# A spectral filter and two MLP layers on one core: chain results taken a tick later, four results in other buffers, stores and sums moved

## The chip, the core and the metric

One core of a Trainium2 chip runs the whole program in one launch. The metric is the device time of that core in microseconds (us), lower is better; it is given as the median of three runs. Engines are named as the profile names them: PE (TensorE, matmuls), DVE (VectorE), ACT (ScalarE), POOL (GpSimd) and SP (SyncE, which only issues transfers here). Transfers are DMAs, issued from the queues of SP, POOL and, at the very end, ACT.

## The reference, cut to what matters

```python
def _attn_ref(x, filt_r, filt_i):             # x: 2 x 3008 x 256
    X = np.fft.rfft(x, axis=1)
    Y = X * (filt_r + 1j * filt_i)[None, :, :]
    return np.fft.irfft(Y, n=x.shape[1], axis=1).astype(np.float32)

def _moe_ref(x, w_in, w_out):                 # 6016 tokens, 256 -> 2048 -> 256
    h = x @ w_in
    return (h * (1.0 / (1.0 + np.exp(-h)))) @ w_out

def _moe2_ref(x, w_gate, w_val, w_out):       # 256 -> 1536 (two of them) -> 256
    g = x @ w_gate
    return ((g * (1.0 / (1.0 + np.exp(-g)))) * (x @ w_val)) @ w_out
```

The output of the filter, as 6016 tokens of 256, goes through `_moe_ref` (layer 1) and the result through `_moe2_ref` (layer 2).

## The kernel before, in words

Every float32 product is made of three matmuls on operands cut into a high and a low part (`PARTS`): high part by an ACT copy, low part by a DVE subtraction. The Fourier transforms come first, then layer 1, then layer 2. The order of the instructions is written out by hand, and each engine runs its own in that order; the framework places the waits. Tiles rotate in pools: `mid` (33 buffers), `u` (4 buffers, pool `tp`), `late` (9 buffers in layer 2), 8 banks of PSUM. A new tile waits until the buffer that it is given has been read, or stored, for the last time.

**Layer 1, last part.** `Wide` handles blocks of 1024 tokens; its second product is `wide_out`. When the last product of a result is made (`end and k == 1`), the result is copied from PSUM to a `u` tile (line 748, ACT; for `m` = 1 of the last block DVE) and stored to DRAM (line 750, by POOL in the last block). The last block has four of these.

**Layer 2** runs on six blocks of 1024 tokens (the last has 896), each in two halves of columns. A block is six units, a unit is one `Pair`: a gate half `g` and a value half `v`, each a `Gate`, which makes a 2 x 2 block product in seven products instead of eight, with additions around them. The steps of a `Gate` that matter here: `p15` (two products; line 873 copies the bank `a` to the bank `y` on ACT, line 876 copies another to `s5`), `p6` (adds a product to `y`; line 891 copies `y` to a `u` tile `u2`), `p3` (line 901, DVE: bank `b` and `u2` summed), `p7` (line 909, DVE: `c` = `y` + `s5`), `p4` (adds a product to `y`, so it may begin only when line 909 has read `y`). The `p4` of the value half is made at the beginning of the next unit (`tail`), after its `p15`. Lines 1027 to 1051 are the activations and the products of gate and value; line 1045 is DVE's first one in the value half. `side(k)`, with k = -1 to 4, are places in a unit where other work is hung: loads of the next operands, their preparation (`prep_x2`, line 809 on POOL) and splitting (lines 796 and 799), loads of weights (line 648) and the output (`store2`: DVE transposes a result, line 1246, and SP issues four stores of it, line 1249). What `later=True` or `lag` puts off is done at the next `side`.

**Layer 2's output product** is woven into this. Units 2c and 2c + 1 make a chain c, 17 in all; a chain has seven products k in the order `ORDER7` = (3, 1, 7, 5, 2, 6, 4), those of `BACK7` = (3, 7, 4) one chain later, each in two parts p. `tick()` is called seven times in a unit; a tick puts three matmuls of one part in a queue (line 1154), and the queue is emptied between the matmuls of the `Gate`s, at least one for two of those. A tick also makes the casts (`high7`, line 1101, ACT), the low parts one tick later (`lower7`, line 1106, DVE), sums of operands by accumulating DMAs on POOL (`more`, line 1088) and loads of weights on SP (`load7`, line 1115). `after7` takes a finished result out of PSUM as soon as the last of its matmuls has been issued: for k = 1 ACT copies the bank to that of k = 6 (line 1129), for the others DVE adds it to an earlier one (line 1127) or, in the first chain of a block, ACT copies it (lines 1140, 1146). The results collect in the tiles `turned`.

**The end.** The last two units do not fit a chain; `product8` makes their plain products (line 1201) in the order of `AT8` after tick `T0`, in four banks, one for each `m` and `l`. A finished bank is added to `turned` by DVE (line 1207), then transposed and stored on SP and ACT. These last ticks have no other products, so a tick is three matmuls there.

Of the kernel before, what the change touches and what calls it, by code (L numbers as in the profile page):

```python
# [29 lines left out]
P = 128  # L30
# [89 lines left out]
def fft_filter_mlp_kernel(  # L120
# [609 lines left out]
    def wide_out(b, f, h):  # L730

        n = WIDE[b] // 2
        w = wt["o1", f // 4, f % 4 // 2]
        end = f == 15

        def one(m, l, k):
            if f == 0 and k == 0:
                acc[0, b, m, l] = psum("acc")
            a = acc[0, b, m, l][:, :n]
            wpart, xpart = PARTS[k]  # L740
            o = 256 * (f % 2) + 128 * m
            nc.tensor.matmul(  # L742
                a, w[:, wpart, o:o + 128], h[xpart][:, n * l:n * l + n],
                start=(f == 0 and k == 0), stop=(end and k == 1), skip_group_check=True,
            )
            if end and k == 1:
                u = tp.tile([P, 512], F32, tag="u", name="x2")
                (nc.vector.tensor_copy if m and b == len(WIDE) - 1 else nc.scalar.copy)(u[:, :n], a)
                eng = nc.gpsimd if b == len(WIDE) - 1 else nc.sync
                eng.dma_start(d3[NSTD + 2 * b + l][:, m, :n], u[:, :n])  # L750

        queue.extend((one, m, l, k) for m in range(2) for k in (0, 2) for l in range(2))
        queue.extend((one, m, l, 1) for m in range(2) for l in range(2))
# [53 lines left out]
    def prep_x2(t, part):  # L807
        x, n = x2_of[t], size2(t) // 2
        sub = lambda o, a, b: nc.gpsimd.tensor_tensor(o, a, b, op=ALU.subtract)
        if part:  # L810
            x[4] = x[2]
            sub(x[4], x[2], x[6])
            return
        r = sp.tile([P, 2, STEP2 // 2], F32, name="s")
        x[5], x[6], x[7] = x["b12"], r[:, 1, :n], r[:, 0, :n]
        sub(x[7], x[3], x["b12"])
        sub(x[5], x["b12"], x[1])
        sub(x[6], x[3], x[5])
# [331 lines left out]
    def product7(c, k, p, i):  # L1150
        n = size2(c // 3) // 2
        o = bank7(c, k)
        wpart, xpart = PARTS[i]
        nc.tensor.matmul(  # L1154
            o, w7[c, k][:, p, wpart], ops7[c, k, p][:, xpart, :n],
            start=(k in (1, 5) and p == 0 and i == 0), stop=(k in (2, 3, 4) and p == 1 and i == 2),
            skip_group_check=True,
        )
        if p == 1 and i == 2:
            after7(c, k)  # L1160

    T0 = 14 * CHAINS
    AT8 = {}
    for p, first in ((0, (2, 3, 6, 7, 8, 9, 10, 11)), (1, range(14, 22))):
        for x, (v, l) in enumerate(((0, 0), (0, 1), (1, 1), (1, 0))):
            for m in range(2):
                AT8[T0 + first[2 * x + m]] = p, v, l, m
    HIGH8 = {}
    for p, first in ((0, (-4, -3, -2, -1)), (1, (2, 3, 4, 5))):
        for x, (v, l) in enumerate(((0, 0), (0, 1), (1, 1), (1, 0))):  # L1170
            HIGH8[T0 + first[x]] = p, v, l

    def raw8(p, v, l):
# [20 lines left out]
    def product8(p, v, l, m, i):  # L1194
        t = NBLK2 - 1
        n = size2(t) // 2
        o = bank(4 + 2 * l + m)[:, :n]
        wpart, xpart = PARTS[i]
        w = w7["8", {(0, 0): 1, (1, 0): 2, (1, 1): 4, (0, 1): 8}[v, m]]
        end = p == 1 and v == (1 if l == 0 else 1)  # L1200
        nc.tensor.matmul(
            o, w[:, p, wpart], ops7["8", p, v, l][:, xpart, :n],
            start=(p == 0 and v == 0 and i == 0), stop=(end and i == 2), skip_group_check=True,
        )
        if end and i == 2:
            a = turned[t, m][:, l, :n]
            nc.vector.tensor_tensor(a, o, a, op=ALU.add)
            store2(t, m, l, (nc.sync, nc.scalar))

    def tick():  # L1210
        i = clock[0]
# [18 lines left out]
        for when, k, j in SUMS:  # L1230
            for p in range(2):
                c, r = divmod(i - when[p], 14)
                if r == 0 and 0 <= c < CHAINS:
                    more(c, k, j, p)
        for r, o in enumerate((-2, 3, 9, 21)):
            c, x = divmod(i - o, 14)
            if x == 0 and 0 <= c < CHAINS:
                load7(c, r)

    turned = {}  # L1240

    def store2(t, m, l, engines=(nc.sync,)):

        n = size2(t) // 2
        o = tp.tile([P, 512], F32, tag="u", name="ob")
        nc.vector.transpose(o[:, :n], turned[t, m][:, l, :n])
        r0 = STEP2 * t + n * l
        for i in range(4):
            engines[i % len(engines)].dma_start(
                out[r0:r0 + n, P * m + 32 * i:P * m + 32 * i + 32].rearrange("(j r) c -> r j c", r=32),  # L1250
                o[32 * i:32 * i + 32, :n].rearrange("p (j c) -> p j c", c=32),
            )


    units = [(1, t, 4 * q + f) for q in range(4) for t in range(2) for f in range(4)]
# [104 lines left out]
    later(0, -1, split_x2, 0, 7)  # L1360
    later(0, 0, split_x2, 0, 4)
    for t in range(1, NBLK2):
        for n, k, m, l in ((3, 2, 0, 0), (3, 4, 0, 1), (4, 2, 1, 1), (5, 2, 1, 0)):
            later(6 * t + n, k, store2, t - 1, m, l)
        u = 6 * t - 6
        later(u + 2, 0, load_x2, t)
# [3 lines left out]

        for k, n in ((1, 2), (4, 3)):
            later(u + 5, k, split_x2, t, n, True)
        later(u + 5, 3, prep_x2, t, 1)
        later(u + 6, -1, split_x2, t, 7, True)
        later(u + 6, 0, split_x2, t, 4, True)

# [32 lines left out]
    with tc.manual_schedule():  # L1409
# [196 lines left out]
        old.finish()  # L1606
        while clock[0] < T0 + 22:
            tick()
            drain(0)


# [39 lines left out]
```

## Time and profile before

| | us |
|---|---|
| median of three runs (1142.25 to 1142.97) | 1142.68 |
| the profiled execution, its own time | 1142.41 |
| its span, first to last instruction | 1140.6 |
| PE busy | 1112.0 |
| DVE busy | 847.0 |
| ACT busy | 773.1 |
| POOL busy | 399.6 |

The page of the profile is one execution. Busy shares are means over stages of different kinds; what ends a stage is seen in the waits (who waited for whom, summed) and in the timeline (instructions in order of time, with the idle time before one and what ended it in brackets). A matmul is drawn longer than the distance to the next one, since they are pipelined. Layer 2 begins at about 590 us; a block is about 89 us, a unit 14 to 15.

### The profile page before, as it was taken

What the parts mean: (1) busy time and instruction counts of PE and PEld (TensorE: products, weight loads), DVE (VectorE), ACT (ScalarE), POOL (GpSimd) and SP (SyncE); (2) the same over time, 40 slices, a digit from 0 to 9 for tenths busy, and PEclk for the clock granted to TensorE, in tenths of its full rate; (3) what the DMA queues carried; (4) which work ended last, traced back from release to release, by engine and by line L of the source; (5) the groups of instructions that cost most, each with busy time, mean ns of one, the idle gap of its engine ahead of it and who ended that gap; (6) DMA issues with size and microseconds to landing.
All of it is one profiled execution on the core that took longest, in us unless ns stands there. A gap on an engine that the chain in (4) does not pass through costs nothing.

```text
span 1140.6 us, 15418 instructions
## 1 busy us (share of the span) xinstructions
PE 1112.0 (97%) x4999; PEld 912.7 (80%) x4999; DVE 847.0 (74%) x1310; ACT 773.1 (68%) x1459; POOL 399.6 (35%) x375
## 2 busy tenths in 40 slices
PE   9999999999999999999998999999999999999996
PEld 7588888998888887888886778778878877887885
DVE  5887465566676686787564788888888888888886
ACT  5788766766676677676564776776676676676662
POOL 3557826544522363352101322322322312322220
PEclk9999999999999999999998999999999999999999
DMA  9974443427254455453673668799799799799794
GB/s 244 289 236 119 135 139 115 145 100 247 100 185 155 151 197 182 148 185 120 212 264 133 137 155 236 180 231 242 172 228 242 193 225 232 201 227 229 194 241 95
DMA packets 146977, 212.70 MB, mean 186 GB/s; under 512 B 58704, under 2 KB 88016, under 8 KB 146896
## 3 DMA queue, kind: packets, MB, share of 16 engines
q1 hardware_dynamic: 125280, 179.26, 49.6%
q0 software_dynamic: 17456, 31.79, 16.2%
q10 hardware_dynamic: 4160, 0.66, 0.3%
q8 instruction: 40, 0.66, 0.2%
q14 instruction: 41, 0.34, 0.1%
HBM read 138.20 MB, written 42.73 MB: 159 GB/s over the span
## 4 chain that ended last, share of the span: by engine, by line
PE 86%; DVE 7%; DMA 3%; ACT 2%; issue 1%; POOL 0%; SPq 0%; DVEq 0%; ACTq 0%
PE bk L840 25%; PE acc L742 15%; PE bk L1154 12%; PE acc L719 7%; PE h L669 6%; PE y L840 6%; PE xb L840 4%; PE xa L840 4%; DMA w<-d 3%; PE s L209 2%; PE s L397 2%; PE s L206 2%; PE s L282 1%; DVE ho L1106 1%; DVE u L901 1%
## 5 line engine op out<-in xcount | busy, mean ns | idle before, releaser
L840 PE MATMUL bk<-xo,wst 128*128 128x512 f32 (+1 forms) x864 | 279.3, 388 | 6.0 <-ACT u L891 3.9
L742 PE MATMUL acc<-h,w 128*128 128x512 f32 x768 | 283.7, 389 | 0.0
L1154 PE MATMUL bk<-ho,w 128*128 128x512 f32 (+1 forms) x714 | 265.5, 388 | 2.0 <-DMA w<-d 2.0
L840 PE MATMUL bk<-xo,w 128*128 128x512 f32 (+1 forms) x648 | 211.7, 393 | 9.4 <-DVE c L909 8.7
L840 PEld LDWEIGHTS bk<-xo,wst 128*128 128x128 f32 x864 | 162.7, 189 | 40.9 <-ACT u L891 4.6
L742 PEld LDWEIGHTS acc<-h,w 128*128 128x128 f32 x768 | 144.2, 188 | 29.6
L1088 POOL DMA_DIRECT2D ga<-c x68 | 59.4, 1063 | 297.1 <-DVE ho L1106 290.4
L1154 PEld LDWEIGHTS bk<-ho,w 128*128 128x128 f32 x714 | 133.9, 188 | 28.4 <-DMA w<-d 4.5
L840 PEld LDWEIGHTS bk<-xo,w 128*128 128x128 f32 x648 | 120.7, 189 | 42.5 <-DVE c L909 18.6
L1106 DVE TENSOR_TENSOR ho<-ga,ho 128x512 fp32r<-128x512 f32 (+1 forms) x136 | 95.2, 701 | 0.6 <-ACT ho L1101 0.6
L719 PE MATMUL acc<-h,w 128*128 128x512 f32 (+1 forms) x384 | 95.4, 376 | 0.0
L1101 ACT CAST ho<-ga 128x512 fp32r<-128x512 f32 (+1 forms) x136 | 82.3, 615 | 6.7 <-PE bk L840 5.3
L669 PE MATMUL h<-xh,w 128*128 128x512 f32 (+1 forms) x248 | 83.6, 379 | 0.1
L719 PEld LDWEIGHTS acc<-h,w 128*128 128x128 f32 x384 | 71.2, 188 | 11.2
L873 ACT COPY bk<-bk 128x512 f32<-128x512 f32 (+1 forms) x72 | 40.7, 566 | 58.0 <-PE bk L840 44.7
L1106 DVE TENSOR_TENSOR ho<-c,ho 128x512 fp32r<-128x512 f32 (+1 forms) x102 | 76.5, 750 | 0.9 <-ACT ho L1101 0.6
L677 DVE TENSOR_TENSOR h<-h,h 128x512 fp32r<-128x512 f32 (+1 forms) x64 | 41.4, 655 | 47.9 <-ACT h L676 46.5
L840 PE MATMUL xb<-xo,wst 128*128 128x512 f32 x192 | 74.7, 391 | 1.6 <-DVE h L936 1.6
L840 PE MATMUL xa<-xo,w 128*128 128x512 f32 x192 | 75.6, 395 | 0.0
L840 PE MATMUL y<-xo,wst 128*128 128x512 f32 x192 | 74.7, 389 | 0.0
L891 ACT COPY u<-bk 128x512 f32<-128x512 f32 (+1 forms) x72 | 41.8, 581 | 40.0 <-PE bk L840 35.2
L901 DVE TENSOR_TENSOR u<-bk,u 128x512 f32<-128x512 f32 (+1 forms) x72 | 48.6, 676 | 18.8 <-PE bk L840 17.4
(165 smaller groups left out, 2193.6 us busy)
## 6 DMA issues: line engine op xcount, KB each, us to landing
w<-d SPq DMA_DIRECT2D x53, 512.0 KB, 4.7
wst<-ds_g SPq DMA_DIRECT2D x36, 512.0 KB, 4.8
wst<-ds_v SPq DMA_DIRECT2D x36, 512.0 KB, 5.1
wst<-ds SPq DMA_DIRECT2D x32, 512.0 KB, 4.6
ga<-c POOLq DMA_DIRECT2D x60, 256.0 KB, 5.6
c<-ga POOLq DMA_DIRECT2D x30, 256.0 KB, 9.1
zt<-d SPq DMA_DIRECT2D x16, 384.0 KB, 5.2
d<-z SPq DMA_DIRECT2D x11, 512.0 KB, 4.4
```

The lines of the kernel that those rows point to most:

```text
L669: nc.tensor.matmul(ps[:, :n], wt[key, f // 4, g][:, wpart, o:o + P], x[xpart][:, g, :n], start=(g == 0 and k == 0), stop=(g == 1 and k == 2),)
L677: nc.vector.tensor_tensor(h[:, 1, :n], u[:, :n], h[:, 0, :n], op=ALU.subtract)
L719: nc.tensor.matmul(a[:, :n], w[:, wpart, o:o + 128], h[:, xpart, :n], start=(f == 0 and k == 0), stop=(f == 15 and k == 2),)
L742: nc.tensor.matmul(a, w[:, wpart, o:o + 128], h[xpart][:, n * l:n * l + n], start=(f == 0 and k == 0), stop=(end and k == 1), skip_group_c ...
L840: nc.tensor.matmul(o, w(wpart), x[:, xpart, :o.shape[-1]], start=(first and k == 0), stop=(last and k == 2), skip_group_check=True,)
L873: nc.scalar.copy(self.y, self.a)
L891: nc.scalar.copy(self.u2, self.y)
L901: nc.vector.tensor_tensor(self.u2, self.b, self.u2, op=ALU.add)
L1088: nc.gpsimd.dma_start(o, v, accum_op=ALU.add)
L1101: nc.scalar.copy(x[:, 0, :v.shape[-1]], v)
L1106: nc.vector.tensor_tensor(x[:, 1, :n], v, x[:, 0, :n], op=ALU.subtract)
L1154: nc.tensor.matmul(o, w7[c, k][:, p, wpart], ops7[c, k, p][:, xpart, :n], start=(k in (1, 5) and p == 0 and i == 0), stop=(k in (2, 3, 4) ...
```

## The change

1. Last block of layer 1: the four results go to `mid` tiles instead of `u` tiles.
2. `after7` is called from the next `tick()` (list `taken`), behind that tick's casts, low parts and sums, and ahead of its loads, instead of straight after the last matmul of a result.
3. `store2` in the blocks but the last: the transposition is put one place of the unit earlier, and the four stores are put off to the next place (`lag`), that is, they stay where they were.
4. `prep_x2`'s last subtraction goes from POOL to DVE and from place 3 to place 4 of its unit.
5. The first load of a chain's weights is issued one tick earlier (-3 instead of -2).
6. The end: the columns' halves are done in the order `ORDER8`; the earlier sum is added to the bank in PSUM (`join8`) between its first and its last products, and the transposition reads the bank.

```diff
--- before.py
+++ after.py
@@ -744,7 +744,10 @@
                 start=(f == 0 and k == 0), stop=(end and k == 1), skip_group_check=True,
             )
             if end and k == 1:
-                u = tp.tile([P, 512], F32, tag="u", name="x2")
+                if b == len(WIDE) - 1:
+                    u = mid([P, 2, 512], "x2")[:, 0]
+                else:
+                    u = tp.tile([P, 512], F32, tag="u", name="x2")
                 (nc.vector.tensor_copy if m and b == len(WIDE) - 1 else nc.scalar.copy)(u[:, :n], a)
                 eng = nc.gpsimd if b == len(WIDE) - 1 else nc.sync
                 eng.dma_start(d3[NSTD + 2 * b + l][:, m, :n], u[:, :n])
@@ -809,7 +812,7 @@
         sub = lambda o, a, b: nc.gpsimd.tensor_tensor(o, a, b, op=ALU.subtract)
         if part:
             x[4] = x[2]
-            sub(x[4], x[2], x[6])
+            nc.vector.tensor_tensor(x[4], x[2], x[6], op=ALU.subtract)
             return
         r = sp.tile([P, 2, STEP2 // 2], F32, name="s")
         x[5], x[6], x[7] = x["b12"], r[:, 1, :n], r[:, 0, :n]
@@ -1157,17 +1160,20 @@
             skip_group_check=True,
         )
         if p == 1 and i == 2:
-            after7(c, k)
+            taken.append((c, k))
+
+    taken = []
 
     T0 = 14 * CHAINS
     AT8 = {}
+    ORDER8 = ((0, 1), (1, 1), (0, 0), (1, 0))
     for p, first in ((0, (2, 3, 6, 7, 8, 9, 10, 11)), (1, range(14, 22))):
-        for x, (v, l) in enumerate(((0, 0), (0, 1), (1, 1), (1, 0))):
+        for x, (v, l) in enumerate(ORDER8):
             for m in range(2):
                 AT8[T0 + first[2 * x + m]] = p, v, l, m
     HIGH8 = {}
     for p, first in ((0, (-4, -3, -2, -1)), (1, (2, 3, 4, 5))):
-        for x, (v, l) in enumerate(((0, 0), (0, 1), (1, 1), (1, 0))):
+        for x, (v, l) in enumerate(ORDER8):
             HIGH8[T0 + first[x]] = p, v, l
 
     def raw8(p, v, l):
@@ -1197,15 +1203,18 @@
         o = bank(4 + 2 * l + m)[:, :n]
         wpart, xpart = PARTS[i]
         w = w7["8", {(0, 0): 1, (1, 0): 2, (1, 1): 4, (0, 1): 8}[v, m]]
-        end = p == 1 and v == (1 if l == 0 else 1)
+        end = p == 1 and v == 1
         nc.tensor.matmul(
             o, w[:, p, wpart], ops7["8", p, v, l][:, xpart, :n],
             start=(p == 0 and v == 0 and i == 0), stop=(end and i == 2), skip_group_check=True,
         )
         if end and i == 2:
-            a = turned[t, m][:, l, :n]
-            nc.vector.tensor_tensor(a, o, a, op=ALU.add)
-            store2(t, m, l, (nc.sync, nc.scalar))
+            store2(t, m, l, (nc.sync, nc.scalar), o)
+
+    def join8(m, l):
+        t = NBLK2 - 1
+        o = bank(4 + 2 * l + m)[:, :size2(t) // 2]
+        nc.vector.tensor_tensor(o, o, turned[t, m][:, l, :o.shape[-1]], op=ALU.add)
 
     def tick():
         i = clock[0]
@@ -1232,24 +1241,36 @@
                 c, r = divmod(i - when[p], 14)
                 if r == 0 and 0 <= c < CHAINS:
                     more(c, k, j, p)
-        for r, o in enumerate((-2, 3, 9, 21)):
+        now, taken[:] = taken[:], []
+        for at7 in now:
+            after7(*at7)
+        for r, o in enumerate((-3, 3, 9, 21)):
             c, x = divmod(i - o, 14)
             if x == 0 and 0 <= c < CHAINS:
                 load7(c, r)
 
     turned = {}
 
-    def store2(t, m, l, engines=(nc.sync,)):
+    def store2(t, m, l, engines=(nc.sync,), src=None):
 
         n = size2(t) // 2
+        if src is None:
+            src = turned[t, m][:, l, :n]
         o = tp.tile([P, 512], F32, tag="u", name="ob")
-        nc.vector.transpose(o[:, :n], turned[t, m][:, l, :n])
+        nc.vector.transpose(o[:, :n], src)
         r0 = STEP2 * t + n * l
-        for i in range(4):
-            engines[i % len(engines)].dma_start(
-                out[r0:r0 + n, P * m + 32 * i:P * m + 32 * i + 32].rearrange("(j r) c -> r j c", r=32),
-                o[32 * i:32 * i + 32, :n].rearrange("p (j c) -> p j c", c=32),
-            )
+
+        def send():
+            for i in range(4):
+                engines[i % len(engines)].dma_start(
+                    out[r0:r0 + n, P * m + 32 * i:P * m + 32 * i + 32].rearrange("(j r) c -> r j c", r=32),
+                    o[32 * i:32 * i + 32, :n].rearrange("p (j c) -> p j c", c=32),
+                )
+
+        if len(engines) > 1:
+            send()
+        else:
+            lag.append(send)
 
 
     units = [(1, t, 4 * q + f) for q in range(4) for t in range(2) for f in range(4)]
@@ -1360,7 +1381,7 @@
     later(0, -1, split_x2, 0, 7)
     later(0, 0, split_x2, 0, 4)
     for t in range(1, NBLK2):
-        for n, k, m, l in ((3, 2, 0, 0), (3, 4, 0, 1), (4, 2, 1, 1), (5, 2, 1, 0)):
+        for n, k, m, l in ((3, 1, 0, 0), (3, 3, 0, 1), (4, 1, 1, 1), (5, 1, 1, 0)):
             later(6 * t + n, k, store2, t - 1, m, l)
         u = 6 * t - 6
         later(u + 2, 0, load_x2, t)
@@ -1370,7 +1391,7 @@
 
         for k, n in ((1, 2), (4, 3)):
             later(u + 5, k, split_x2, t, n, True)
-        later(u + 5, 3, prep_x2, t, 1)
+        later(u + 5, 4, prep_x2, t, 1)
         later(u + 6, -1, split_x2, t, 7, True)
         later(u + 6, 0, split_x2, t, 4, True)
 
@@ -1606,6 +1627,9 @@
         old.finish()
         while clock[0] < T0 + 22:
             tick()
+            for i, m, l in ((11, 0, 1), (12, 1, 1), (13, 0, 0), (14, 1, 0)):
+                if clock[0] == T0 + i + 1:
+                    join8(m, l)
             drain(0)
```

## Rows read from the trace of the kernel before

**Rows 1.** Waits of PE, whole span: us in total, times, longest.

```profile
PE bk L840 <- DVE c L909: 8.7, 7, 1.5
PE bk L840 <- ACT u L891: 3.9, 1, 3.9
PE bk L1154 <- DMA w<-d: 2.0, 4, 0.9
...
PE bk L840 <- ACT bk L873: 1.2, 2, 0.8
...
PE bk L840 <- ACT ho L1101: 0.8, 1, 0.8
```

**Rows 2.** Timeline at the transition: start, duration, instruction, idle before and its releaser.

```profile
607.17 0.59 ACT L891 COPY u<-bk 128x512 f32<-128x512 f32 x1 [4.59 <-DMA d<-x]
...
607.81 0.80 PE L840 MATMUL bk<-xo,wst 128*128 128x512 f32 x1 [3.92 <-ACT u L891]
```

**Rows 3.** Windows after it: length, busy by engine (PE first), PEclk, DMA.

```profile
607.80:613.80 6.00, 5.99 (x14) 4.73 (x15) 3.22 (x5) 1.16 (x2) 0.00 (x0) 0.51 0.11 40
613.80:619.80 6.00, 6.00 (x27) 4.80 (x26) 2.24 (x5) 4.57 (x9) 0.91 (x1) 1.00 0.41 147
```

**Rows 4.** Timeline at the end of unit 11 (DVE, POOL, PE).

```profile
757.76 0.69 DVE L1127 TENSOR_TENSOR oa<-bk,s 128x512 f32<-128x512 f32 x1 [1.64 <-PE bk L1154]
...
758.37 0.68 DVE L799 TENSOR_TENSOR xo<-x,xo 128x512 fp32r<-128x512 f32 x1
...
759.19 1.29 POOL L809 TENSOR_TENSOR x<-x,s 128x512 f32<-128x512 f32 x1 [3.92 <-issue]
...
759.59 1.44 DVE L1106 TENSOR_TENSOR ho<-ga,ho 128x512 fp32r<-128x512 f32 x1
...
763.50 0.39 PE L1154 MATMUL bk<-ho,w 128*128 128x512 f32 x1
...
764.08 0.68 DVE L1127 TENSOR_TENSOR s<-bk,oa 128x512 f32<-128x512 f32 x1
...
764.68 0.68 DVE L909 TENSOR_TENSOR c<-bk,s 128x512 f32<-128x512 f32 x1
...
765.42 0.98 PE L840 MATMUL bk<-xo,w 128*128 128x512 f32 x3 [1.53 <-DVE c L909]
```

**Rows 5.** Waits of DVE for chain products, whole span.

```profile
DVE oa L1127 <- PE bk L1154: 53.0, 38, 2.6
```

**Rows 6.** Timeline of DVE, SP and PE around a late weight load.

```profile
729.00 0.70 DVE L1246 STREAM_TRANSPOSE ob<-oa 128x512 f32<-128x512 f32 x1
...
729.73 2.75 SPq L1249 DMA_DIRECT2D out_dram<-ob  x4
...
733.53 1.25 SPq L1115 DMA_DIRECT2D w<-d  x1
...
741.42 0.50 PE L1154 MATMUL bk<-ho,w 128*128 128x512 f32 x1 [0.37 <-DMA w<-d]
```

**Rows 7.** Timeline of ACT and PE in unit 11.

```profile
753.68 0.57 ACT L1129 COPY bk<-bk 128x512 f32<-128x512 f32 x1 [0.54 <-PE bk L1154]
...
756.86 0.58 ACT L873 COPY bk<-bk 128x512 f32<-128x512 f32 x1
...
757.56 0.66 PE L840 MATMUL bk<-xo,wst 128*128 128x512 f32 x2
```

**Rows 8.** Timeline of PE in unit 12.

```profile
772.89 0.50 PE L840 MATMUL bk<-xo,w 128*128 128x512 f32 x1
```

**Rows 9.** Timeline of the end: PE, SP, DVE.

```profile
1117.82 2.88 PE L1154 MATMUL bk<-ho,w 128*128 128x448 f32 x12 [0.91 <-DMA w<-d]
...
1127.83 5.03 PE L1201 MATMUL bk<-ho,w 128*128 128x448 f32 x24
...
1132.40 4.44 SPq L1249 DMA_DIRECT2D out_dram<-ob  x8
...
1135.30 0.65 DVE L1246 STREAM_TRANSPOSE ob<-oa 128x448 f32<-128x448 f32 x1
```

## The prediction

> **What bounds the kernel now.** The summary of the profile gives TensorE (PE) busy nearly all the time, so I read only where PE stops. First view: the waits of PE, summed by releaser [rows 1]. The largest sum is for line 909, the DVE addition that makes `c` out of PSUM; then one single wait of 3.9 us for line 891, then waits for chain weights (`w<-d`), then two for line 873. Second view: the timeline around one of each. These stalls lie in three places, and each has its own cause.
>
> Place one is the step from layer 1 to layer 2. The last block of layer 1 copies four results into tiles of tag `u`, of which there are four, and GpSimd stores them. The next `u` tiles, those of layer 2, get a buffer only when a store has landed: ACT's copy at line 891 waits 4.59 us for `d<-x`, and PE sits idle for 3.92 us [rows 2]. The granted clock is 0.51 in the 6 us after that and 1.00 in the 6 us after those: 14 matmuls against 27 [rows 3]. Place two is the end of the last pair of each block (units 5, 11, 17, 23, 29 and 35): PE ends a chain product at 763.50 and starts again at 765.42, waiting for line 909 at 764.68 [rows 4]. Place three is a late weight load: SP issues four output stores at 729.73, just after DVE's transposition at 729.00, the load behind them goes out at 733.53 and its product starts late at 741.42 [rows 6].
>
> How I count a stall: matmuls start 6.00/27 = 0.22 us apart [rows 3] but are drawn 0.39 long, so an idle time of 1.53 is a gap of 765.42 - 763.50 = 1.92 between starts, 1.70 lost [rows 4]; the first matmul after a stop takes 0.50 instead of 0.39 [rows 6, 8], another 0.11. A stall costs its idle time plus about 0.28.
>
> **Part 1: layer 1's last results in other buffers.** The four copies take `mid` tiles, and the `u` ring is free. What hides the new allocations: `mid` has 33 buffers, the wide pairs' `h` tiles are just being given back there, and the stores that hold the four are short; I cost the allocation at nothing, and at the whole stall if it has to wait. Removed: the idle 3.92 and the 0.17 by which a matmul is drawn longer than its place (0.39 - 0.22), 4.1 us, and the slow clock, 27 - 14 = 13 matmuls of 0.22 = 2.9 us [rows 2, 3]. After the idle 1.53 of [rows 4] three matmuls take 0.98 us, full speed, so without a longer gap I expect no fall. Late next is the sum at line 909 of the first pair, with 0.1 to 0.3 us. Gain 6.6 (0 to 7.0).
>
> **Part 2: chain results one tick later.** Seven ticks make a pair of 63 products: 63 x 0.222 = 14.0 us, a tick is 2.0 us. Today a result is taken in DVE's queue straight after its last product is issued, so DVE waits for PE: 53.0 us in 38 waits [rows 5], 1.64 of it at 757.76, at the busiest pair of the block [rows 4]. From there DVE runs without a pause to 765.4, and another result, at 764.08, stands just ahead of line 909 [rows 4]. Deferred, the first falls behind two conversions that are ready, so the 1.64 disappears; the second falls behind line 909's product. The tail of that queue also has a conversion of 1.44 us instead of 0.68, beside GpSimd's subtraction at 759.19 [rows 4]; that subtraction moves to DVE and behind line 909, which gives 0.76 and costs 0.6 later. Together 1.64 + 0.6 + 0.76 = 3.0 us, against a stall of 1.5: DVE is then ready first, by up to 1.5 us, and line 909 waits for PE. Removed: six idle times, 8.7 less a seventh of 0.2, 8.5 in sum, plus 6 x 0.28 = 10.2; I keep 0.1 for each and take 9.6 (5 to 10.2) [rows 1]. Some 7 us later in five blocks there is a second, small stall at 772.89, again a matmul of 0.50 [rows 8]; two slow starts and an idle of 0.1, with what a drawn matmul hides, make it up to 0.5; the deferred result and the subtraction come into that stretch (two more operations, 1.2 us) while DVE enters it up to 1.5 us earlier. Between 0 and 2.5 for the five; I take 1.5.
>
> What the wait costs elsewhere: ACT takes some results too. Line 1129 (the copy from one bank to another) sits at 753.68 in a gap in which ACT has nothing else; a tick later it stands among the casts before line 873 (756.86), which then ends 0.5 later [rows 7]. Behind it is PE: `v.p6` starts at 757.56, line 873 ends at 757.44, so 0.12 us is left and about 0.4 of the 0.5 becomes a stall, plus a slow start: 0.5. This holds in five blocks (unit 35, with fewer casts, has room) and once more in unit 3, where line 873 already stalls PE [rows 1]: -3.0. In unit 4 the other stall by line 873 shrinks, because a result leaves the casts ahead of it: +0.3. Sum -2.7 (0 to -6). A bank held one tick longer costs nothing: by the order `ORDER7` its next writer is four or more ticks away.
>
> **Part 3: output transpositions one place earlier, their stores at the old place, one weight load a tick earlier.** The store instructions keep their place in SP's queue, but the data they wait for is ready one place, about 2 us, earlier; the loads `wst` and `w` behind them follow. The load of [rows 6] then lands about 2 us sooner against a stall of 0.37 + 0.28. Three such waits (of the four in rows 1 the fourth is in the tail), one of 0.8 that the view gives to a cast but which stands at the same place of its block, and a small one in the last block, which the view does not list and which I put at 0.5: 1.1 + 0.8 + 4 x 0.28 + 0.5 = 3.5. I take 3.0 (0 to 3.5). The earlier first load passes one `wst` load, which is wanted a pair later. DVE's second transposition now stands ahead of line 909 in units 9, 15, 21, 27 and 33: 0.6 us more in that queue, 0 to -0.3 each for PE, and I take nothing, because none of the long waits of [rows 1] stands at that place.
>
> **Part 4: the end.** The last block's wait for weights, 0.91 + 0.28 [rows 9], has out stores ahead of it in the same way; but DVE converts without a pause in this stretch, so PE catches up with it: +0.8 (0 to 1.2). After the last matmul (1127.83 + 5.03 = 1132.86) DVE today does four additions and four transpositions in turn until 1135.95 [rows 9]. With the sum already made in PSUM only the transposition of the last is left, 0.65 us: 1133.7, 2.2 us sooner; and with the columns' order changed two of the four outputs are ready 12 matmuls earlier. The eight issues on SP take 4.4 us [rows 9], so the stores may bind in place of DVE; begun 1.7 us earlier, they would end 1.7 earlier. I take 2.0 (1.7 to 2.2). The additions go into DVE's idle time while PE works on other banks, which is free as long as DVE is done within three to five ticks of 0.6 us. The trace has no transposition that reads PSUM; the nearest rows are operations that read it (0.69 at 757.76) and that don't (0.68 at 758.37) [rows 4], so I price it as before, 0.65. [...]
>
> **The sum**, on the profiled execution of 1142.4 (span 1140.6 and 1.8 around it; the median of the runs is 0.3 higher): 6.6 + 9.6 + 1.5 - 2.7 + 3.0 + 0.8 + 2.0 = 20.8, so 1121.6, and 1121.9 against the median; I put it between, at 1121.8.
>
> **Rivals.**
> (a) The transition keeps its stop: a `mid` buffer comes free late, or PE stops for something else and the clock falls again. For it: pools are emptied and filled just there, and loads for layer 2 take `mid` tiles too. Against: ACT's row names `d<-x` alone [rows 2]. Part 1 is lost: 1128.5. Chance 0.10.
> (b) The wait is moved, not removed: deferred results and the subtraction push the next sum at line 909 or line 873 over its limit, as 0.12 us of room at 757.56 shows is possible [rows 7]. Half of 9.6 + 1.5 lost and the ACT cost doubled: 1121.8 + 5.5 + 2.7 = 1130. Chance 0.14.
> (c) Slower: the later reading holds a PSUM bank beyond its next writer. Price: one tick for each of 17 chains, 17 x 2.0 = 34.7, beside the gains left, 20.8: about 1156. It decides from the point where a bank is rewritten within one tick of its last product; the order by hand says four ticks, and in the tail, where ticks are 0.6 us, DVE is the one who could be late. Chance 0.02.
> (d) The change does not reach these waits (they have another last releaser): 1142.5. Chance 0.02.
> (e) No cost appears and every stall goes: 28 us, 1115. Chance 0.04.
>
> **How the numbers follow.** The forecast, 0.68, has 1117 to 1126 for its own. With (a) and most of (b) the range is 1116.5 to 1130. Faster or slower means by over 0.2%, about what a measurement of this kernel tells from none: faster 0.96, same 0.02, slower 0.02.
>
> **What would show it.** Right: no PE wait for line 891 near 604 and a clock of 1.00 there; DVE's waits for chain products down from 53 us to under 15; no PE wait over 0.5 us for line 909; no wait for `w<-d` over 0.3; new PE waits of about 0.4 us for line 873 in units 5, 11, 17, 23, 29; the last transposition within 1 us of the last matmul. Wrong: a stop of over 2 us at the transition, line 909 still among the first of PE's waits, or loads that land late although the stores were issued earlier.

## The result: 1142.5 us before, 1127.1 us after

The changed kernel takes 1127.13 us (median; 1126.51 to 1127.43), the kernel before 1142.47 in the runs beside it (1141.98 to 1142.97). The ratio is 0.9865, 95% interval 0.9848 to 0.9882. The profiled execution of after is 1127.43 with a span of 1125.7, so 15.0 us less than the profiled execution of before; the prediction's sum was 20.8. In the new file the lines behind 748 stand 3 further down: line 909 is now 912, 873 is 876, 891 is 894, 1106 is 1109, 1115 is 1118, 1127 is 1130, 1129 is 1132, 1154 is 1157; the transposition is line 1260, an output store line 1265.

The waits of PE in after (us in total, times, longest), against [rows 1]:

```profile
PE bk L843 <- ACT bk L876: 2.9, 7, 1.3
PE bk L843 <- DMA wst<-ds_g: 2.1, 2, 1.2
PE bk L843 <- DVE c L912: 1.9, 3, 1.0
...
PE bk L1157 <- DMA w<-d: 0.9, 1, 0.9
```

The wait for line 891 is gone and that for line 909 fell from 8.7 to 1.9. But the bank copy of line 873 has grown from 1.2 to 2.9, and a wait is new that the prediction had not counted: `wst`, the weights of the gate half.

The transition in after, as windows (length, busy by engine, PE first, then PEclk, DMA share and GB/s), against [rows 3]:

```profile
600.00:606.00 6.00, 6.00 (x28) 4.96 (x27) 3.33 (x6) 3.39 (x7) 2.37 (x4) 1.00 0.99 343
606.00:612.00 6.00, 5.87 (x26) 4.54 (x25) 3.61 (x7) 3.73 (x7) 0.00 (x0) 1.00 0.94 347
```

DVE's waits for chain products in after, against [rows 5]:

```profile
DVE oa L1130 <- PE bk L1157: 1.4, 2, 1.0
```

PE makes 28 and 26 matmuls in two windows of 6 us at a granted clock of 1.00; before, it stood still for 3.92 us and then made 14 at 0.51 [rows 2, 3]. DVE's waits fell from 53.0 us to 1.4.

**The account.** In both timelines I took the distances between the starts of successive matmuls of layer 2 over their usual ones (0.227 us for 512 columns, and 0.199 for 448, the lower end of 0.199 to 0.207 there), listed each that is over by more than 0.05, and added the slow starts behind a stop to it (at 763.98 in after, behind line 912, the first matmul is drawn 0.50 us long in place of 0.39). Two stalls of 0.40 early in layer 2, the same in both, are left out. Single slow starts of 0.1 behind no idle time (0.9 before, 0.4 in after) are counted with the small stalls and the late `w`.

| place | lost before | lost after | gain | predicted |
|---|---|---|---|---|
| transition, with a new first wait at line 912 | 6.97 | 0.46 | 6.51 | 6.6 |
| ends of units 5, 11, 17, 23, 29 (line 909) | 8.68 | 0 | 8.68 | 8.0 |
| end of unit 35 (line 909) | 1.59 | 1.23 | 0.36 | 1.6 |
| five second, small stalls (line 909) | 3.09 | 2.62 | 0.47 | 1.5 |
| three other small ones by line 909, one by 891 | 0.93 | 0 | 0.93 | 0 |
| ACT's lines 873 and 891 | 1.78 | 5.25 | -3.47 | -2.7 |
| `w` late, all but the last wait | 3.89 | 0 | 3.89 | 3.0 |
| `w` late, the last wait, in the last block | 1.37 | 1.20 | 0.17 | 0.8 |
| unit 27 (line 912), new | 0 | 1.02 | -1.02 | 0 |
| `wst` late, units 28 and 34, new | 0 | 2.62 | -2.62 | 0 |
| last matmul to end of span | 7.74 | 5.87 | 1.87 | 2.0 |
| stages before layer 2, and amounts under 0.05 | | | -0.84 | 0 |

The column of gains sums to the 14.9 between the spans. The large terms came as worked out; of the 5.8 us that are missing from the sum of 20.8, 3.6 are the two new stalls.

### The profile page after: what moved, and what is told of

Read it like the earlier page. It is cut to its first block, busy times and chain, and to the rows that moved or that the text cites. A ratio compares the mean times of both kernels' runs of the same rounds, so it can differ in the third digit from the quotient of the medians.

```text
span 1125.7 us, 15425 instructions
## 1 busy us (share of the span) xinstructions
PE 1107.8 (98%) x4999; PEld 912.2 (81%) x4999; DVE 847.4 (75%) x1316; ACT 772.2 (69%) x1459; POOL 391.6 (35%) x369
## 4 chain that ended last, share of the span: by engine, by line
PE 86%; DVE 6%; ACT 3%; DMA 2%; issue 2%; POOL 0%; SPq 0%; DVEq 0%; ACTq 0%
PE bk L843 25%; PE acc L742 15%; PE bk L1157 11%; PE acc L719 7%; PE h L669 6%; PE y L843 6%; PE xb L843 4%; PE xa L843 4%; PE s L206 2%; PE s L397 2%; PE s L209 2%; DMA wst<-ds_g 1%; PE s L282 1%; ACT ho L1104 1%; DVE ho L1109 1%
## 5 line engine op out<-in xcount | busy, mean ns | idle before, releaser
L843 PE MATMUL bk<-xo,w 128*128 128x512 f32 (+1 forms) x648 | 208.9, 389 | 2.5 <-DVE c L912 1.9
L1109 DVE TENSOR_TENSOR ho<-c,ho 128x512 fp32r<-128x512 f32 (+1 forms) x102 | 72.6, 712 | 0.7 <-ACT ho L1104 0.6
```

The costliest lines, as they stand in the source:

```text
L843: nc.tensor.matmul(o, w(wpart), x[:, xpart, :o.shape[-1]], start=(first and k == 0), stop=(last and k == 2), skip_group_check=True,)
L1109: nc.vector.tensor_tensor(x[:, 1, :n], v, x[:, 0, :n], op=ALU.subtract)
```

## The experiments

All were timed beside the kernel before, whose medians in the three groups were 1142.56 (e1 to e4, e5 to e8) and 1143.11 (e9 to e12). So a difference of 0.6 us or so between runs of different groups is not clear; the ratios take out what the groups differ by.

| kernel | median us | ratio to before, 95% interval |
|---|---|---|
| after | 1127.13 | 0.9865 (0.9848 to 0.9882) |
| e1, transition alone | 1136.40 | 0.9949 (0.9934 to 0.9964) |
| e2, results at once | 1125.26 | 0.9857 (0.9839 to 0.9876) |
| e3, bank copy at once | 1123.06 | 0.9832 (0.9817 to 0.9846) |
| e4, first load back | 1124.59 | 0.9846 (0.9832 to 0.9861) |
| e5, subtraction back | 1124.10 | 0.9839 (0.9824 to 0.9854) |
| e6, both back | 1130.96 | 0.9895 (0.9880 to 0.9910) |
| e7, e3 and e4 together | 1121.66 | 0.9814 (0.9797 to 0.9830) |
| e8, three more places | 1122.63 | 0.9825 (0.9810 to 0.9840) |
| e9, e3, e4 and e5 together | 1119.09 | 0.9789 (0.9774 to 0.9803) |
| e10, end back | 1128.67 | 0.9872 (0.9855 to 0.9888) |
| e11, e4 and stores back | 1124.30 | 0.9836 (0.9821 to 0.9851) |
| e12, e9 and POOL freed | 1117.64 | 0.9775 (0.9760 to 0.9789) |

### Part 1 by itself (e1)

Before, with the first hunk of the change alone:

```diff
-                u = tp.tile([P, 512], F32, tag="u", name="x2")
+                if b == len(WIDE) - 1:
+                    u = mid([P, 2, 512], "x2")[:, 0]
```

> The kernel before with part 1 alone: the last block's four results of layer 1 in `mid` tiles. Theory (the buffer of tag `u` is the whole cause of the stop and of the slow clock): no wait for line 891 near 604, granted clock 1.00 in the 12 us behind it, and 6.5 us less than the kernel before, about 1136.0; all other waits as in the kernel before. Rival (time won at the transition runs into the loads of layer 2 and is given back): the waits for `wst` or `x2` tiles behind 610 grow, and 0 to 4 us are left, 1138.5 to 1142.5.

Measured: 1136.40, 6.2 less; PEclk is 1.00 in the windows from 600 to 612, with 27 and 26 matmuls. The buffer was the cause of the stop and of the slow clock, and nothing of the gain is given back at the place. Some of it moves later: two waits for `wst` (1.8 us) stand where `w` had waited.

### The ends of the units: which of two edits (e2, e5, e6)

The prediction gave the end of a unit to two edits at once: results read a tick later, and the last subtraction of `prep_x2` moved from POOL to DVE. Three kernels take them apart; with after they are a table of two by two.

```diff
 e2:
-            taken.append((c, k))
+            after7(c, k)
 e5:
-            nc.vector.tensor_tensor(x[4], x[2], x[6], op=ALU.subtract)
+            sub(x[4], x[2], x[6])
-        later(u + 5, 4, prep_x2, t, 1)
+        later(u + 5, 3, prep_x2, t, 1)
 e6: both
```

> The kernel after with the chain results taken at once again (part 2 without its later reading; the subtraction stays on DVE). Theory (the later reading is what frees DVE at the ends of the units): DVE waits about 50 us for chain products again, PE's six waits for the sum at line 912 come back with 1.0 to 1.5 us each, 1.3 to 1.8 lost, 9 in sum, while the stalls by the bank copy of line 876 (five of 0.58, and 0.6 in unit 3) go: 1127.1 + 9 - 3.5 = 1132.6. Rival (moving the subtraction from POOL to DVE was what freed the ends of the units): no such waits, only the bank copy's stalls go: 1123.6.

> The kernel after with the last subtraction of the operands' preparation back on POOL and at its old place; chain results stay a tick later. Theory S (the subtraction beside DVE is what held the units' ends; it came up with the run in which results were taken at once): the waits at line 912 come back at the ends of units 5, 11, 17, 23, 29, up to 1.7 lost at each: 1127.1 + 5 x 1.7 = 1135.6. Theory E (either of the two edits is enough at that place): no such waits, 1127 to 1128.5. Theory D (the prediction's: the later reading gives most of it, the subtraction 0.76 of 3.0): a small part of the waits, 0.2 to 0.5 each, 1128 to 1129.5.

> The kernel after with both undone: results taken at once, and the subtraction on POOL at its old place. Theories S, E and D alike have the waits at line 912 back at the five ends of units, 1.7 each, against the run with only the results at once (1125.3): 1133.8. By S it is 1 to 2 us below the run with the subtraction alone put back, since the later reading costs ACT's stalls; by E and D it is 5 us or more above that run.

| median us | subtraction on POOL | on DVE |
|---|---|---|
| results at once | 1130.96 | 1125.26 |
| a tick later | 1124.10 | 1127.13 |

Either edit alone is worth 5.7 to 6.9 us. The second one costs 1.9 to 3.0: at the ends of the units it is an either-or (theory E). e2 beat its expectation by 7 us, since its theory had the waits come back; e6 came 2.8 below its own, since the waits came back with 1.2 us each and not 1.5. The end of unit 11 in the four, from the timelines of DVE, POOL and PE, first e6:

```profile
750.84 0.69 DVE L1130 TENSOR_TENSOR oa<-bk,s 128x512 f32<-128x512 f32 x1 [1.16 <-PE bk L1157]
...
752.65 1.79 DVE L1109 TENSOR_TENSOR ho<-c,ho 128x512 fp32r<-128x512 f32 x1
...
757.48 0.68 DVE L912 TENSOR_TENSOR c<-bk,s 128x512 f32<-128x512 f32 x1
...
752.27 1.62 POOL L812 TENSOR_TENSOR x<-x,s 128x512 f32<-128x512 f32 x1 [3.91 <-issue]
...
758.22 0.73 PE L843 MATMUL bk<-xo,w 128*128 128x512 f32 x2 [1.22 <-DVE c L912]
```

In e2, the subtraction on DVE:

```profile
751.76 0.68 DVE L1109 TENSOR_TENSOR ho<-c,ho 128x512 fp32r<-128x512 f32 x1
...
755.49 0.68 DVE L912 TENSOR_TENSOR c<-bk,s 128x512 f32<-128x512 f32 x1
...
756.33 0.86 PE L843 MATMUL bk<-xo,w 128*128 128x512 f32 x3
```

In e5, the results a tick later:

```profile
748.57 1.77 DVE L1109 TENSOR_TENSOR ho<-c,ho 128x512 fp32r<-128x512 f32 x1
750.26 0.68 DVE L1130 TENSOR_TENSOR oa<-bk,s 128x512 f32<-128x512 f32 x1
750.99 0.69 DVE L1048 SCALAR_TENSOR_TENSOR ga<-bk,ga 128x512 f32<-128x512 f32 x1
...
753.52 0.68 DVE L912 TENSOR_TENSOR c<-bk,s 128x512 f32<-128x512 f32 x1
```

In after, both:

```profile
752.63 0.69 DVE L1048 SCALAR_TENSOR_TENSOR ga<-bk,ga 128x512 f32<-128x512 f32 x1 [1.16 <-PE bk L843]
...
757.72 0.68 DVE L815 TENSOR_TENSOR x<-x,s 128x512 f32<-128x512 f32 x1
...
763.25 0.68 DVE L912 TENSOR_TENSOR c<-bk,s 128x512 f32<-128x512 f32 x1
```

In e6 DVE waits 1.16 us for a result and then spends 1.79 on an operation that takes 0.68 where POOL is quiet; PE idles 1.22. Taking away the 1.1 beside POOL (e2) clears the idle time, in all blocks but for 0.1 to 0.3; taking away the wait (e5) clears it in all, although line 1109 is still 1.77 long. With both (after) DVE stands idle for 1.16 ahead of line 1048: that is the surplus. And it has a price: the subtraction at 757.72 is another 0.6 in a stretch that DVE runs through without a pause until the next line 912 at 763.25, behind which PE loses 0.43. In e5 these five second stalls are not there at all (0.3 of single slow starts is left); the row costs 2.6 in after, 3.2 in e2 and 3.3 in e6. The other price, of the later reading, is ACT's copy: e3, the next kernel, reads that one result at once and all others a tick later, and at 1123.06 it is 2.2 below e2. So beside the subtraction on DVE the later reading of the other results still wins something; what it costs in after is the copy.

### ACT's copy (e3) and the first load (e4)

```diff
 e3:
+            if k == 1:
+                after7(c, k)
+            else:
-            taken.append((c, k))
+                taken.append((c, k))
 e4:
-        for r, o in enumerate((-3, 3, 9, 21)):
+        for r, o in enumerate((-2, 3, 9, 21)):
```

> The kernel after, but ACT's copy from bank to bank (k = 1) is made at once again, all other results a tick later. Theory (that copy, standing among the casts, is what delays line 876): the five stalls of 0.40 to 0.45 and 0.12 in units 5, 11, 17, 23, 29, the one of 0.39 and 0.12 in unit 27/28 and 0.6 of the 1.6 in unit 3 go: 5 x 0.57 + 0.5 + 0.6 = 4.0 less, 1123.1. Rival (PE is held there by the next thing in the queue, the copy `u` of line 894 or a cast): the stall stays under another name, 1126 to 1127.5.

> The kernel after with the first weight load of a chain at its old tick (-2). Theory (a tick earlier this load waits for a buffer on SP, and the load `wst` for the gate half stands behind it): the two waits of 1.35 and 1.14 us for `wst` near 1003 and 1086 go, 2.6 less, 1124.5, if no wait for `w` returns; with the waits of 0.4 for `w` in the blocks back, 4 x 0.6 are lost again and the time stays at 1127. Rival (the stores that now stand one after the other ahead of both loads hold them up): the waits for `wst` stay as they are, 1127.

Measured: 1123.06 and 1124.59, both as the theory had them. After in unit 11, timeline of ACT and PE:

```profile
747.76 0.58 ACT L1132 COPY bk<-bk 128x512 f32<-128x512 f32 x1
...
749.83 0.58 ACT L876 COPY bk<-bk 128x512 f32<-128x512 f32 x1
...
750.46 0.74 PE L843 MATMUL bk<-xo,wst 128*128 128x512 f32 x2 [0.28 <-ACT bk L876]
```

After ahead of unit 28's products with `wst`, timeline of SP and PE:

```profile
996.33 0.34 SPq L1118 DMA_DIRECT2D w<-d  x1
996.77 0.37 SPq L648 DMA_DIRECT2D wst<-ds_g  x1
...
1004.49 0.47 PE L843 MATMUL bk<-xo,wst 128*128 128x512 f32 x1 [1.17 <-DMA wst<-ds_g]
```

SP's waits at the chain's weight loads (us, times, longest), in after:

```profile
SPq L1118 <- PE bk L1157: 148.3, 26, 25.0
```

and in e4:

```profile
SPq L1118 <- PE bk L1157: 98.8, 24, 9.4
```

The copy stands in the queue ahead of the casts, and line 876 ends 0.5 later. In e3 all seven waits but the one of unit 3 are gone, which is 0.8 idle, as before. The first load of a chain takes the buffer of a weight tile that a product still reads; a tick earlier SP waits longer for it (148.3 us against 98.8, one wait of 25.0 against 9.4), and `wst`, which stands behind it, goes out at 996.77 and comes 1.17 too late. In e4 there is no wait for `wst` among the first of PE's, and none for `w` in any block but the last (0.24).

### Which edit brought the weights in time (e11)

e4, with `store2` at its old places and its stores sent straight after the transposition:

```diff
-        for n, k, m, l in ((3, 1, 0, 0), (3, 3, 0, 1), (4, 1, 1, 1), (5, 1, 1, 0)):
+        for n, k, m, l in ((3, 2, 0, 0), (3, 4, 0, 1), (4, 2, 1, 1), (5, 2, 1, 0)):
-            lag.append(send)
+            send()
```

> The kernel after with the first weight load at its old tick (1124.6 so far) and the output transpositions and stores as in the kernel before: old places, sent at once. Theory (stores that wait for their transposition hold up SP's queue, and the loads behind it): the waits for `w` in four blocks are back, 0.4 to 1.0 lost in each, and the one near 1103 grows: 2.5 to 3.5 more, 1127.5. Rival (with the other edits in place the loads come in time anyway): 1124 to 1125.

Measured: 1124.30 against 1124.59 in e4, no difference, and no wait for `w` above 0.01 us: the rival's time, and not the theory's 1127.5. The earlier transpositions and the stores put off do nothing once the other parts are there. Why shows in unit 9 of e11 (timeline of DVE and SP), beside [rows 6]:

```profile
721.64 0.70 DVE L1260 STREAM_TRANSPOSE ob<-oa 128x512 f32<-128x512 f32 x1
...
725.71 0.71 SPq L1118 DMA_DIRECT2D w<-d  x1
```

Counted from line 1011 of the unit (716.31; in before line 1008, at 722.03) the transposition comes after 5.33 us, before after 6.97: 1.64 sooner at the same place. In before a chain result is read just ahead of it (DVE's timeline):

```profile
728.39 0.69 DVE L1127 TENSOR_TENSOR oa<-bk,s 128x512 f32<-128x512 f32 x1 [0.42 <-PE bk L1154]
```

With its wait that is 1.0 of the 1.64, and part 2 takes it away. The load follows, 9.40 against 11.50.

The reverse holds too. e6 has part 3 as it is in after, but takes the results at once, and DVE waits for them again (53.0 us before):

```profile
DVE oa L1130 <- PE bk L1157: 43.7, 37, 2.4
```

Its unit 9 (timeline of DVE and SP):

```profile
720.45 0.69 DVE L1260 STREAM_TRANSPOSE ob<-oa 128x512 f32<-128x512 f32 x1
...
723.85 0.36 SPq L1118 DMA_DIRECT2D w<-d  x1
```

Counted from line 1011 (715.69) the transposition comes after 4.76 us and the load after 8.16, both sooner than in e11, and among PE's waits in e6 there is none for `w`. So either the later reading or part 3 is enough for the weights; after has both.

### Unit 27, and the combinations (e7, e8, e9, e12)

The timeline of after in unit 27 (DVE, POOL, PE), where POOL prepares the last block (448 columns), and at its end the same meeting one block earlier (512 columns):

```profile
976.94 2.96 DVE L1109 TENSOR_TENSOR ho<-c,ho 128x512 fp32r<-128x512 f32 x1
...
981.39 0.68 DVE L912 TENSOR_TENSOR c<-bk,s 128x512 f32<-128x512 f32 x1
...
977.48 1.86 POOL L812 TENSOR_TENSOR s<-x,x 128x448 f32<-128x448 f32 x1
979.42 1.50 POOL L812 TENSOR_TENSOR x<-x 128x448 f32<-128x448 f32 x1
...
982.12 0.50 PE L843 MATMUL bk<-xo,w 128*128 128x512 f32 x1 [0.75 <-DVE c L912]
...
889.95 0.68 DVE L1109 TENSOR_TENSOR ho<-c,ho 128x512 fp32r<-128x512 f32 x1
...
890.49 2.01 POOL L812 TENSOR_TENSOR s<-x,x 128x512 f32<-128x512 f32 x1
```

A DVE operation of 0.68 takes 2.96 and runs through POOL's first subtraction into the second. Line 912 at 981.39, which reads PSUM, takes 0.68 in the midst of POOL's third (981.00, 1.46 long).

```diff
 e7: e3 and e4            e9: e3, e4 and e5
 e8: e7 and
-        later(u + 3, 1, prep_x2, t, 0)
+        later(u + 3, -1, prep_x2, t, 0)
         (in the very last unit)
+            v.p7()                      # ahead of the product of lines 1052 to 1054
         (chain 15, last weight load: two ticks earlier)
 e12: e9, the same move of p7, and
-        sub = lambda o, a, b: nc.gpsimd.tensor_tensor(o, a, b, op=ALU.subtract)
+        sub = lambda o, a, b: (nc.gpsimd if part or t == 0 else nc.vector).tensor_tensor(...)
-        later(u + 3, 1, prep_x2, t, 0)
+        later(u + 2, 3, prep_x2, t, 0)
```

> The kernel after with two edits together that each helped alone: the bank copy (k = 1) at once, the first weight load at its old tick. Theory (the two are independent, on ACT and on SP): 4.0 + 2.5 less than after, 1120.6; no wait for line 876 above 0.3 behind 640, none for `wst` above 0.3. Rival (the faster kernel brings the loads behind their users again): 1122 to 1123, with a wait for `w` or `wst` in some blocks.

> The run before this one (copy at once, load at its old tick) with three more edits at three places that stalled: POOL's three subtractions of the next block's operands moved from place 1 to place -1 of their unit; in the very last unit the product `p7` and its sum at line 912 ahead of the product of gate and value; the last weight load of chain 15 two ticks earlier. Theory (in unit 27 DVE is held by POOL's subtractions, 2.96 us for a 0.68 us operation; in unit 35 line 912 stands behind other work of DVE; the load of chain 15 stands behind output stores on SP): the waits of 0.9 near 980, of 1.1 near 1099 (half of it) and of 0.4 to 1.0 near 1103 go: 1.0 + 0.55 + 0.5 less, 1118.5. Rival for unit 27 (the 2.96 us is a wait inside DVE for something else than POOL): the long operation stays at its place though the subtractions have gone, and 1.0 of it is not won.

> The kernel after with three of its edits undone that each made it faster when undone alone: the last subtraction back on POOL at its old place (3.0 less alone), the bank copy (k = 1) at once (4.0 less alone), the first weight load at its old tick (2.5 less alone). Theory (three causes on three engines, which add up): 1127.1 - 9.5 = 1117.6; of PE's waits behind 640 only those near 980, 1099 and 1103 are left above 0.3. Rival (the second and third meet the same stall as the first, or loads come late): 1119 to 1121.

> The run with three edits undone (expected 1117.6) with two more edits: the three subtractions that POOL made beside the busiest pair, 977 to 982 in unit 27, are made by DVE one unit earlier, in a pause of DVE (967.8 to 970.1 there); in the very last unit the product `p7` and line 912 stand ahead of the product of gate and value. Theory (POOL's subtractions hold DVE in unit 27, other work of DVE holds line 912 in unit 35): 1.0 and 0.45 less, 1116.2, and no operation of DVE's line 1109 above 1.2 us in units 27. Rival (the pause is not there in all blocks, or the operands land too late): DVE waits for line 774's loads, and PE for line 1048 or 912; 1118 or more.

e7 came to 1121.66, 1.1 above its sum by the medians (by the ratios it has 0.0051 of 0.0052), and with one of the late loads that its rival needs: the last block's `w` costs 0.95 of idle time where e4 has 0.24. e8 missed by 4: the long operation of unit 27 is 1.17 there and line 912 no longer stops PE, so POOL's subtractions were the cause. But three of POOL's accumulating DMAs, issued from 975.52 on in after, now stand behind them (980.50), and other waits come up (waits of PE in e8, whose lines are another 3 further down):

```profile
PE bk L1160 <- DMA w<-d: 1.9, 4, 0.8
...
PE bk L1160 <- DVE s L1133: 1.2, 1, 1.2
```

The first row is four late weight loads; that the delayed DMAs of POOL hold them up was not tried by itself. The second is in the last block: with its weights there in time, PE waits for DVE to read the bank of the result before. That is the mechanism of the prediction's rival (c), 1.2 us in one place. In after the weights still come last there.

e9 is 1119.09, at the edge of its rival's range: 8.0 of the 9.6 that e3, e4 and e5 win one by one (by the spans 8.8 of 10.8, by the ratios 0.0076 of 0.0078). Behind 640 only units 27 and 35 and the last block have idle times of PE above 0.2. e12 takes out the first and part of the second and is the fastest, 9.5 below after. Its waits of PE, those of layer 2:

```profile
PE bk L843 <- ACT bk L876: 0.8, 1, 0.8
PE bk L843 <- DVE c L912: 0.5, 1, 0.5
```

and the first of DVE's three subtractions in its timeline, unit 26:

```profile
962.22 0.62 DVE L812 TENSOR_TENSOR s<-x,x 128x448 f32<-128x448 f32 x1
```

The three take 0.62 each, in a pause of DVE; POOL needed 1.46 to 1.86 for one.

### The end (e10)

After with the old order of the columns, and the sums behind the last matmuls:

```diff
-    ORDER8 = ((0, 1), (1, 1), (0, 0), (1, 0))
+    ORDER8 = ((0, 0), (0, 1), (1, 1), (1, 0))
-            store2(t, m, l, (nc.sync, nc.scalar), o)
+            a = turned[t, m][:, l, :n]
+            nc.vector.tensor_tensor(a, o, a, op=ALU.add)
+            store2(t, m, l, (nc.sync, nc.scalar))
         (the calls of join8 are left out)
```

> The kernel after with the old end: columns in the old order, four sums and four transpositions behind the last matmuls. Theory (DVE's sums bind at the end): 1.9 more, 1129.0, and from the last matmul to the span's end 7.7 us in place of 5.9. Rival (issues of stores on SP and ACT bind): under 0.8 more, 1127.1 to 1127.9. If a transposition that reads PSUM costs more than one that does not, it shows in the same run: 0.65 us is the row for 448 columns out of SBUF.

Measured: 1128.67, 1.5 more (0.8 by the ratios). The end of after (timeline of PE and DVE):

```profile
1114.71 5.12 PE L1207 MATMUL bk<-ho,w 128*128 128x448 f32 x24
...
1119.25 1.27 DVE L1260 STREAM_TRANSPOSE ob<-bk 128x448 f32<-128x448 f32 x2 [1.21 <-DMA out_dram<-ob]
```

and of e10:

```profile
1114.42 5.02 PE L1207 MATMUL bk<-ho,w 128*128 128x448 f32 x24
...
1121.89 0.65 DVE L1262 STREAM_TRANSPOSE ob<-oa 128x448 f32<-128x448 f32 x1
```

The transpositions of 448 columns, grouped by line and form (busy us, mean ns, idle before), in after, out of PSUM:

```profile
L1260 DVE STREAM_TRANSPOSE ob<-bk 128x448 f32<-128x448 f32 x4 | 2.5, 650 | 1.8 <-DMA out_dram<-ob 1.2 <-PE bk L1207 0.6
```

and in e10, out of SBUF:

```profile
L1262 DVE STREAM_TRANSPOSE ob<-oa 128x448 f32<-128x448 f32 x4 | 2.6, 645 | 0.1
```

DVE ends 0.69 us behind the last matmul in after (1120.52 - 1119.83) and 3.10 in e10 (1122.54 - 1119.44). Of these 2.4 the time shows 0.8 to 1.5, which lies between the rival's bound of 0.8 and the theory's 1.9 and does not decide. From the last matmul to the end of the span it is 5.9 us in after and 9.4 in e10, where the theory had 7.7; but e10's profiled execution, 1130.64, is the slowest of its four by 1.8. From PSUM a transposition takes 650 ns, from SBUF 645, which is 0.005 us apart.

## Why the prediction was right, and where it was not

**Transition: right**, in place, mechanism and size: 6.6 predicted, 6.5 in the account, 6.2 in e1; line 912 came next, as said.

**Ends of units: right in outcome, with a step missing in the working.** Five stalls went (8.7 against 8.0). The sum "1.64 + 0.6 + 0.76 = 3.0 us, against a stall of 1.5" has terms of the right order (1.16 of waiting and 1.1 beside POOL in e6), and the prediction says itself that DVE is then "ready first, by up to 1.5 us"; that surplus is 1.16 of idle time in after. The step that is missing is the one behind it: that either edit then does by itself, and the other brings its cost. The prediction put the subtraction's cost at "0.6 later", and let the second small stalls shrink by 1.5 all the same: this term was mis-sized. They shrank by 0.5 and are gone, another 2.6, in e5, where the subtraction is elsewhere.

**Unit 35: wrong step**, "six idle times". The sixth is of another kind: after `p7` of the very last unit PE has hardly anything but the product that needs line 912, and DVE goes from line 1048, which waits for PE (1097.55), through three more operations to line 912, which ends at 1100.44. No reading of a result stood between them in after, and 1.23 is still lost. Moving line 912 one operation up gave 0.4 (e12: 0.51 idle where after has 0.95).

**ACT's cost: right in place and mechanism**, 3.5 against 2.7; five stalls of 0.5 and 0.5 in unit 3, as said, one more of 0.5 in unit 27, which was not, and 0.2 in place of 0.3 back in unit 4. e3 shows that it need not have been paid: this copy is on ACT, and nothing that it delayed there stood ahead of line 909.

**Weights: the outcome right, the step one of two that do.** The loads came in time (3.9 gained, 3.0 predicted). Part 3, on which the prediction counts, is enough by itself in e6, where DVE still waits; but e11 has none of it and is in time as well, because DVE no longer waits. The prediction did not see that its part 2 does the same work. The step that failed with a loss is "The earlier first load passes one `wst` load, which is wanted a pair later", which counted the load's place in the queue, and not that it might wait there for its buffer: -2.6, won back in e4.

**Unit 27: not foreseen.** The prediction knew that DVE is slow beside POOL's subtraction (1.44 us in place of 0.68, [rows 4]) and moved only that one out of the way; the other three now met DVE at another moment.

In after, two operations of line 1109, whose inputs `c` and `ho` are both in SBUF, took 2.96 and 1.04 us beside POOL's subtractions there; lines 904 and 912, which read a bank of PSUM, took 0.68 each beside them (979.82 and 981.39). As far as the starts on POOL, which are rough in the profile, can be trusted, they do not tell when DVE is held: at 976.94 it started 0.54 ahead of POOL and took 2.96, at 889.95 it also started 0.54 ahead and took 0.68.

**End: right** (1.9 against 2.0 in the account; 0.8 to 1.5 by e10). A sum in it is wrong: 1132.86 + 0.65 is 1133.5 and not 1133.7, so DVE could gain 2.4 and not 2.2; it gained 2.4, and the time less. **Last block: wrong step**, "+0.8": its weights come as late as before (0.88 idle, before 0.91).

**What was to show it**: the transition, DVE's waits (1.4, under 15), line 873 in five units (0.22 to 0.28 idle for the 0.4 named) and the last transposition (0.69) as said; line 909 with 0.75 and 0.95, and `w` with 0.88, over their bounds. The 28 us of rival (e), where every stall goes, are more than the upper bounds in the working add up to, 26.6.

Open: why DVE is held in unit 27 (2.96 us) and not in units 9, 15 and 21 at the same distance (0.68 in each, 0.54 ahead of POOL), and whether e9 stays short of the sum of its three parts at all (1.6 us by the medians, nothing clear by the ratios).

## What to carry to other kernels

Two edits that relieve the same wait do not add up: find how long the stall is, take the cheaper edit, and count what the second one costs where its work goes. To see which one did it, undo both as well as each: with one undone the other still hides the wait, and neither seems to do anything. Of results that are read later, put off only those whose reader waits and holds up others; and before a load is issued earlier, see whether its buffer is free by then: here SP's longest wait at the chain's weight loads was 9.4 us in e4 and 25.0 in after, where a `wst` load that stood behind one came 1.17 us too late. A stall that looks like five others in the summed waits may have another cause at the last place: look at each one's own timeline.

## What the runs showed of the hardware

A DVE subtraction of 128x512 took 2.96 us in place of 0.68 beside POOL's subtractions of 128x448 (after, 976.94). A POOL subtraction took 1.64 to 2.01 us for 512 columns in unit 21 and 1.46 to 1.86 for 448 in unit 27, while the same of 448 columns on DVE took 0.62 (e12): three of POOL's, put into a pause of DVE, cost 1.86 us there, less than the 2.28 for which DVE had been held. Four output stores of the same shape took SP 1.96 us to issue in one place (before, 759.70) and 6.09 in another (after, 986.61). After the 3.92 us stop PE had 6 us at a clock of 0.51 (before, 607.80). Behind shorter idle times in layer 2, of up to 1.53 us in before from 618 on and up to 1.34 in after, the granted clock was 1.00 in every window of 6 us or less to the last matmul.
